# Four interleaved layers on one core: tokens of both parities side by side in a tile, part of the hi/lo split on TensorE, and a schedule written out in tables

## The chip, the cores and the metric

One core of one Trainium2 chip. The metric is device microseconds of one execution; a kernel's time is the median of its runs. The engines are called as in the profile: PE (TensorE matmul), PEld (its weight loads), DVE (VectorE), ACT (ScalarE), POOL (GpSimd) and SP (SyncE, which here only issues DMAs).

## What is computed

S = 2048 tokens of D = 512 features pass through four layers, each with a residual: A, B, A, B, with the same weights for both A and for both B.

```python
def _A_ref(x, wqkv, wo):            # H = 32 heads of 16, W = 8 keys, dilation 2
    q, k, v = split_heads(x @ wqkv)
    idx = pos[:, None] - 2 * arange(8)[None, :]      # keys t, t-2, ..., t-14
    logits = einsum("bhsd,bhswd->bhsw", q, k[idx]) * Dh ** -0.5   # masked where idx < 0
    return einsum("bhsw,bhswd->bhsd", softmax(logits), v[idx]) @ wo
def _B_ref(x, w1, w2, w3, w4):      # F = 1792
    h = gelu(layernorm(x) @ w1)
    g = [h's quarters of features, shifted by +1, -1, +2, -2 tokens]
    x1 = x + concat(g) @ w2
    return x1 + gelu(layernorm(x1) @ w3) @ w4
x = x + _A_ref(layernorm(x)); x = x + _B_ref(layernorm(x))    # twice
```

## The kernel before

**Blocks and tiles.** The tokens are cut into four blocks of 512 (`NB`), each block into four tiles of 128 (`NT`), and there are two layer pairs, so stages run over n = 0 to 7: n = 4*l + b. Tile i of a block holds the tokens 8k + 2i + par (k = 0 to 63, par 0 or 1) of that block. Partition p = 64*par + k: the even ones in the lower half, the odd ones in the upper. A token's eight keys then lie in the same partition or in its neighbours of the same half.

**hi/lo split.** Matmuls run in fp16 with every operand as two halves, an early one (the value rounded to fp16, "hi") and a late one (the rest, "lo"); `HLS` lists the three products hi*hi, hi*lo, lo*hi. So a product with 512 features in takes 12 matmuls of 128x512. Block 0's QKV product and the first MLP (n = 0) are in fp32 instead, because the weights are not split yet.

**Stages.** `p1_stream(n)` normalises a block's tiles, transposes them on PE, splits them and multiplies by the QKV weights; results go through the buffers `ev` (three) to DRAM (`kv_d`, `q_d`). `p2_unit(n, qt)` is the attention of a quarter of the features (8 heads) of a block: it loads q and, for K and for V, 11 slots of 128 features per partition, and works on DVE: a product of 4096 elements per partition, a reduction, the softmax (the exponential on ACT), a second product, three adds. `p3(n)` multiplies by Wo, normalises, transposes and splits, multiplies by W1 and writes the mixer's input `h`, transposed, with short copies on POOL for the shifts across its columns. `p4(n)` multiplies by W2 and normalises, `p5(n)` is the MLP in 14 chunks of 128 of F, with the weights' halves read from DRAM (`w34`), where `big_pair` put them. A tile's transpose and split is `turn_pe` (line 644): four transposes into one PSUM tile, then `split` (line 667): ACT copies the early half out, DVE subtracts it from the PSUM tile and writes the late half.

**Block 0.** Its Q, K and V stay in SBUF: `p1_quarters` writes them there, and `p2_unit` (lines 946 to 966) copies and shifts K and V by SBUF-to-SBUF DMAs, one copy and four shifts for each of K and V and each quarter; the last rows go to `kv_d` for block 1.

**Transfers.** `dma` (line 473) is one DMA from SP; `dma2` (line 477) is two, one for each half of the partitions. Loads of x and of kv and stores of K and V go half by half.

**What sets the order.** Nothing is issued where it is written. Every step is an operation in a graph, `op(key, alts, ...)` (class `Graph`, line 201), with its engine and an assumed duration, or several engines to choose from. `plan` (line 246) runs a small event model: whenever an engine is free, it gives it the ready operation with the lowest key whose buffers are free, and takes the buffers that are free. The keys written in the code are overridden by the table `PLACES` (line 57). An operation that only some engines may do takes the engine that comes free first in that model. The order that results is kept on each engine (`InOrder`, line 348), and each engine runs its queue strictly in order. Since every instruction is issued through `InOrder`, the profile gives them all line 358; the tiles tell them apart.

Some names of tiles in the profile: `xt` the transposed input of QKV, `nT` the transposed input of W1 or W3, `oT` the attention's output transposed, `prod` the attention's products, `L` its logits, `f` normalised tiles, `g` the MLP's middle, `acc` its sums, `mm` the other PSUM tiles (four).

Of the kernel before, what the change touches and what calls it, by code (L numbers as in the profile page):

```python
# [18 lines left out]
P = 128  # L19
# [11 lines left out]
PAD = W - 1  # L31
NSL = NT + W - 1
# [6 lines left out]

# [4 lines left out]


PLACES = [int(k) for k in """
# [127 lines left out]
""".split()]  # L185


class Buf:

# [11 lines left out]
class Graph:  # L201
# [3 lines left out]
    def __call__(self, key, alts, r=(), w=(), after=(), xfer=0.0):  # L205
# [26 lines left out]
        for p in before:  # L232
            p.succ.append(o)
# [1104 lines left out]
```

## Time and profile before

| what | value |
|---|---|
| median of 3 runs | 1242.08 us (1238.16 to 1244.62) |
| span of the profiled execution | 1238.3 us |
| its own time | not given beside the span; the lowest run is 1238.16 us |
| PE / DVE / ACT / POOL busy | 1193.5 / 903.5 / 632.0 / 372.4 us |
| instructions | 15802 |
| moved by DMA | 176.71 MB in 129597 packets |

The span runs from the first to the last instruction. A busy PE may be running at half clock: the column PEclk of a stretch is the mean clock that it was granted, as a share of the full one. In a row of waits stand the total, how often, and the longest. In a row of a timeline stand start, duration, engine, line, operation, tiles, count, and in brackets the idle time before it with what ended it; SPq is a DMA's issue on SP.

### The profile page before, as it was taken

How to read it: one execution, taken by the hardware profiler on the slowest of the kernel's cores; microseconds unless marked ns; L12 is line 12 of the kernel's file. 1: busy time of each engine (PE TensorE's matmuls, PEld its weight loads, DVE VectorE, ACT ScalarE, POOL GpSimd, SP SyncE). 2: the span in 40 equal slices, each digit the busy share in tenths (PEclk: the TensorE clock that was granted, in tenths of full speed). 3: DMA queues.
4: the chain of work that ended last, by engine and by line, in shares of the span. 5: the costliest groups of instructions: out<-in, count | busy, mean ns of one | idle time of the engine just before them, and what ended most of it. 6: DMA issues, size and time to landing. Idle time of an engine off the chain costs nothing.

```text
span 1238.3 us, 15802 instructions
## 1 busy us (share of the span) xinstructions
PE 1193.5 (96%) x5676; PEld 592.2 (48%) x5676; DVE 903.5 (73%) x896; ACT 632.0 (51%) x1108; POOL 372.4 (30%) x516
## 2 busy tenths in 40 slices
PE   9977799899999999999999999989999999999998
PEld 7533344455454445444444545444454444444554
DVE  4776998998999989599954998389855888314212
ACT  4645547533774456556543655365543654444431
POOL 6342123402540264147422252051513432121000
PEclk9988899899999999999999999999999999999999
DMA  6565777586666543653348623764157435211322
GB/s 199 160 163 156 220 219 227 161 227 169 195 178 177 132 136 81 151 154 95 109 147 197 162 75 126 202 153 124 60 153 187 124 93 167 68 60 58 88 85 68
DMA packets 129597, 176.71 MB, mean 143 GB/s; under 512 B 11504, under 2 KB 72912, under 8 KB 129520
## 3 DMA queue, kind: packets, MB, share of 16 engines
q1 hardware_dynamic: 127216, 173.78, 50.2%
q10 hardware_dynamic: 2304, 1.95, 0.6%
q8 instruction: 44, 0.72, 0.3%
q14 instruction: 33, 0.27, 0.1%
HBM read 132.64 MB, written 37.87 MB: 138 GB/s over the span
## 4 chain that ended last, share of the span: by engine, by line
PE 76%; DVE 7%; DMA 7%; ACT 3%; POOL 2%; SPq 2%; issue 2%; ACTq 0%; DVEq 0%; POOLq 0%
PE mm L358 54%; PE acc L358 22%; DVE prod L358 3%; SPq L358 2%; DMA kv<-kv_d 2%; DMA kv<-x 1%; DVE L L358 1%; POOL b L358 1%; DMA w<-in_A_x_dram 1%; POOL a L358 1%; DMA h<-in_B_w_dram 1%; ACT junk L358 1%; DMA q<-q_d 1%; ACT ev L358 1%; DMA kv_d<-ev 1%
## 5 line engine op out<-in xcount | busy, mean ns | idle before, releaser
L358 PE MATMUL acc<-w,g 128*128 128x512 f16 (+1 forms) x1260 | 309.0, 394 | 0.0
L358 PE MATMUL mm<-nT,w 128*128 128x512 f16 (+1 forms) x1288 | 305.5, 390 | 1.5 <-ACT nT L358 0.7
L358 PE MATMUL mm<-wq_hl,xt 128*128 128x512 f16 x1008 | 234.8, 389 | 13.3 <-ACT ev L358 11.4
L358 ACT ACTIVATE mm<-mm,s_w 128x512 f32<-128x512 f32 (+1 forms) x144 | 90.6, 629 | 228.8 <-PE mm L358 228.5
L358 PEld LDWEIGHTS <-w 128*128 128x128 f16 x1344 | 124.9, 98 | 137.3 <-issue 1.3
L358 PEld LDWEIGHTS <-g 128*128 128x128 f16 x1176 | 115.1, 98 | 129.9 <-issue 1.1
L358 PEld LDWEIGHTS <-xt 128*128 128x128 f16 x1008 | 100.3, 100 | 133.8 <-issue 23.2
L358 DVE TENSOR_TENSOR prod<-kv,q 128x4096 f32<-128x4096 f32 x29 | 128.6, 4434 | 20.2 <-DMA kv<-kv_d 12.2
L358 DVE TENSOR_TENSOR prod<-kv,L 128x4096 f32<-128x4096 f32 x32 | 141.4, 4418 | 0.6 <-DMA kv<-kv_d 0.3
L358 DVE TENSOR_REDUCE L<-prod 128x256 f32<-128x4096 f32 x32 | 141.2, 4414 | 0.1
L358 DVE TENSOR_TENSOR prod<-prod 128x2048 f32<-128x2048 f32 x64 | 117.5, 1837 | 1.1
L358 POOL TENSOR_TENSOR g<-f,g 128x512 f16<-128x512 f32 x42 | 61.0, 1453 | 189.7 <-ACT g L358 89.4
L358 DVE SCALAR_TENSOR_TENSOR g<-mm,c_g,g 128x512 f16<-128x512 f32 x56 | 41.8, 747 | 75.8 <-ACT g L358 74.1
L358 PE MATMUL mm<-nT,w_hl 128*128 128x512 f16 x384 | 87.8, 379 | 0.0
L358 PE MATMUL mm<-wo_hl,oT 128*128 128x512 f16 x384 | 86.1, 379 | 0.0
L358 PE MATMUL mm<-w_hl,h 128*128 128x512 f16 x384 | 85.0, 379 | 0.0
L358 POOL COPY h<-h 128x126 f16<-128x126 f16 (+3 forms) x56 | 47.4, 869 | 118.1 <-DVE h L358 116.6
L358 PE MATMUL mm<-ident,f 128*128 128x128 f32 x384 | 59.0, 280 | 21.0 <-ACT f L358 16.0
L358 ACT ACTIVATE g<-mm,c_g 128x512 f16<-128x512 f32 x98 | 66.9, 685 | 2.1
L358 PEld LDWEIGHTS mm<-ident,f 128*128 128x128 f32 x384 | 47.2, 143 | 40.2 <-ACT f L358 19.1
L358 ACT ACT_TABLE_LOAD x48 | 61.6, 1283 | 9.0 <-DVE mx L358 5.2
L358 PEld LDWEIGHTS <-oT 128*128 128x128 f16 x426 | 41.7, 98 | 49.4 <-issue 0.6
(159 smaller groups left out, 1365.0 us busy)
## 6 DMA issues: line engine op xcount, KB each, us to landing
w<-w SPq DMA_DIRECT2D x196, 256.0 KB
kv<-kv_d SPq DMA_DIRECT2D x112, 352.0 KB
w<-in_B_w_dram SPq DMA_DIRECT2D x56, 256.0 KB
kv_d<-ev SPq DMA_DIRECT2D x112, 128.0 KB
x<-x SPq DMA_DIRECT2D x32, 256.0 KB
q_d<-ev SPq DMA_DIRECT2D x28, 256.0 KB
w<-g SPq DMA_DIRECT2D x28, 256.0 KB
q<-q_d SPq DMA_DIRECT2D x28, 256.0 KB
```

Source lines behind the costliest of these rows:

```text
L358: i = f(*a, **k).ins
```

## The change

- **Parities side by side.** Partition p = 2k + par. The rows of a tile of x then are one access pattern, and every transfer that went half by half is one DMA. K, V and Q share one DRAM tensor `kvq_d`, 12 planes (K, V, Q times four quarters), with four rows of zeros ahead of each. A kv load takes 12 slots in three pieces of 512 floats per partition, rows p, p+2 and p+4.
- **Block 0.** Quarters 1 to 3 of its K and V are stored to `kvq_d` and loaded back like those of other blocks; quarter 0 is shifted in SBUF by three DMAs each for K and V.
- **h.** Its columns are permuted so that the shifts are reads of 128 columns next to each other; the writes to the first two quarters become strided by pairs.
- **Split on PE.** `turn_split(minus=True)` multiplies the early half by minus the identity into the PSUM tile with the transposes, and ACT copies the late half out. It is taken for n in `MINUS`: the QKV inputs of n = 1 to 3 and the W1 inputs of n = 0 and 1. Elsewhere the subtraction stays on DVE. A third form by transposing DMA (`turn_dma`) is written but `BY_DMA` is empty.
- **Finer operations, more engines.** The softmax steps and the adds of an attention unit, and the PSUM copies of block 0, are operations of their own; more kinds have two or three engines to choose from.
- **Tables.** `PLACES`, the durations and the event model are gone. `ORDER` lists all 3135 operations (number times 4, plus the engine's place among the alternatives), `SLOTS` gives each buffer its place.
- The statistics of blocks 1 to 3 come ahead of their tiles (`p1_stats`), with one power for four tiles (`powers`). Explicit dependencies, such as Wo after the previous W2, go.

The core of the diff (`...` marks what is left out):

```diff
-PAD = W - 1
-NSL = NT + W - 1
+NSL = NT + W
+BACK = 4
...
+ORDER = [int(k) for k in """
+40 8 12 24 28 1492 32 20 1476 16 56 0 52 4 60 36 64 472 100 48 464 44 468 104 70 80 768 72 776 76 110 84 461 112 488
...
 def plan(ops, slots):
...
+    for b, c in zip(bufs.values(), "".join(SLOTS.split()), strict=True):
+        b.t = slots[b.kind][int(c, 16)]
+    for k in ORDER:
+        o = ops[k // 4]
+        assert o.before | o.order <= done
+        done.add(o)
+        todo.append(o.alts[k % 4][1])
+    assert len(done) == len(ops)
+    return todo
...
-    kv_d = [dram.tile([3, 4, 2, PAD + S // 2, P], F32, name=f"kv_d{l}") for l in range(2)]
-    q_d = [dram.tile([4, NB, P, NT, P], F32, name=f"q_d{l}") for l in range(2)]
+    minus_id = const.tile([P, P], F16, name="minus_id")
+    G.tensor_scalar(minus_id, ident, -1.0, None, ALU.mult)
+    kvq_d = [dram.tile([12, BACK + S // NT, NT * P], F32, name=f"kvq_d{l}") for l in range(2)]
...
+    def turnstile(line, *a):
+        before[line] = [dma(*a, after=before.get(line, ()))]
...
-    def rows(ap, b, i, par):
+    def rows(ap, b, i):
+        v = ap[512 * b + 2 * i:512 * b + 2 * i + 1, 0:D]
+        return at(v, [[8 * D, 64], [D, 2], [1, D]])
...
-        dma2(key, lambda p: par_of(f32v(t.t, D), p), lambda p: rows(x_d, b, i, p), [], [t], 0.8, after)
+        dma(key, lambda: f32v(t.t, D), lambda: rows(x_d, b, i), [], [t], after)
...
+    def turn(key, n, dst, rd):
         ps = Buf("mm")
         def fn():
             for c in range(NC):
                 f = slice(P * c, P * (c + 1))
-                T.transpose(ps.t[:, f], n.t[:, f], ident)
+                T.matmul(ps.t[:, f], n.t[:, f], ident, is_transpose=True, start=(c == 0), stop=(c == NC - 1))
...
+    def turn_split(key, n, dst, cells, hi, lo, rd, scale=None, minus=False):
+        ps, pv = turn(key, n, dst, rd)
+        hc, lc = [(dst, [(c, a) for c in cells]) for a in range(2)]
+        if minus:
+            act(key, lambda: A.activation(hi(), pv(), AF.Copy), [ps], [hc])
+            pe(key, lambda: T.matmul(pv(), minus_id, hi(), start=False, stop=True, skip_group_check=True), [hc], [ps])
+            act(key, lambda: A.activation(lo(), pv(), AF.Copy), [ps], [lc])
+        elif scale is None:
+            act(key, lambda: A.activation(hi(), pv(), AF.Copy), [ps], [hc])
+            dve(key, lambda: V.tensor_sub(lo(), pv(), hi()), [ps, hc], [lc])
...
+    MINUS = (1, 2, 3), (0, 1), ()
+    BY_DMA = (), (), (), ()
...
-                    for par in range(2):
-                        dma(key, lambda i=i, j=j, par=par: at(
-                            kv_d[l][j - 1, 0, par, PAD + 256 * b + i], [[NT * P, 64], [QS, 4], [1, P]]),
...
+                dma(key, lambda i=i, k=k: at(
+                    kvq_d[l][4 * k, BACK + P * b, P * i:P * (i + 1)], [[RS, P], [QS, 4], [1, P]]),
...
+                turnstile("kv", kl + 0.12 * j, lambda j=j: kv[j].t.rearrange("p (s f) -> p s f", s=3),
+                          lambda j=j: at(plane(l, j, qt, P * b), [[RS, P], [2 * RS, 3], [1, RS]]),
+                          [(kvb[l], [(*c, j) for c in cells] + ["pad"])], [kv[j]])
...
+            def to(a, g=g):
+                v = blocks(h.t, HW)[:, a, g]
+                if g < 2:
+                    return at(v[:, 1:], [list(v.ap[0]), [P, NT], [2, 64], [P - 1, 2]])
+                return v[:, P:] if g == 2 else v[:, :D]
...
-                for p in range(2):
-                    dma(base, lambda b=b, i=i, p=p: rows(out_d, b, i, p),
-                        lambda x=x, p=p: par_of(x.t, p), [x], [], 0.4, by_act=n == N - 1 and p == 1)
+                dma(base, lambda b=b, i=i: rows(out_d, b, i), lambda x=x: x.t, [x], [], by_act=n == N - 1 and k % 2)
```

More of the change, by code (lines that the diff above doesn't have):

```diff
@@ L193, in __init__ @@
         self.kind, self.t, self.cells = kind, t, {}
-        self.users, self.left, self.slot = 0, 0, None
 class Op:
-    __slots__ = ("key", "alts", "succ", "n", "est", "touch", "seq", "fn", "end", "xfer", "eng", "lend")
+    __slots__ = ("alts", "before", "order", "touch", "seq")
 class Graph:
@@ L231, in __call__ @@
         before.discard(o)
-        for p in before:
-            p.succ.append(o)
-        o.n = len(before)
+        o.before, o.order = before, set(after)
         o.touch = [b for b in touch.values() if b.kind is not None]
-        for b in o.touch:
-            b.users += 1
-            b.left += 1
         self.ops.append(o)
         return o
-LAT, LAT_PE, LAT_SP, LAT_DMA, TABLE = 0.12, 0.4, 0.3, 2.3, 1.3
 def plan(ops, slots):
-    free = [0.0] * 5
-    pool = {k: [(0.0, j) for j in range(len(v))] for k, v in slots.items()}
+    bufs, done, todo = {}, set(), []
@@ L439, in tile_mixer @@
     V.memset(nhalf, -0.5)
-    maskb = const.tile([P, NT, W], F32, name="maskb")
-    G.memset(maskb, 0.0)
-    for base in (0, 64):
-        for i in range(NT):
-            if i < 3:
-                G.memset(maskb[base:base + 2, i, 0:3 - i], -1e9)
-            G.memset(maskb[base:base + 1, i, 0:7 - i], -1e9)
+    junk = const.tile([P, D], BF16, name="junk")
+    zero = slots["prod"][0][:4 * 8, :D]
+    V.memset(zero, 0.0)
     ident = const.tile([P, P], F32, name="ident")
@@ L468, in tile_mixer @@
+    RS = NT * P
+    QS = (BACK + S // NT) * RS
     kvb = [Buf() for _ in range(2)]
-    qb = [Buf() for _ in range(2)]
     w34 = Buf()
-    def dma(key, out, in_, r, w, xfer, after=(), by_act=False):
-        e, q, d = (ACT, A, 0.6) if by_act else (SP, Y, 0.45)
-        return op(key, [(e, d, lambda: q.dma_start(out(), in_()), None)], r, w, after, xfer)
-    def dma2(key, out, in_, r, w, xfer, after=()):
-        def fn():
-            for par in range(2):
-                Y.dma_start(out(par), in_(par))
-        return op(key, [(SP, 1.15, fn, None)], r, w, after, xfer)
@@ L500, in tile_mixer, with act, dve, gp @@
-    GELU, EXP = "gelu", "exp"
-    xd1 = [dram.tile([P, NT, D], F32, name=f"x1_{b}") for b in range(NB)]
+    def act(key, fn, r, w, cls=None, after=(), also=()):
+        return op(key, [(ACT, fn, cls), *also], r, w, after)
+    def dve(key, fn, r, w, after=(), also=()):
+        return op(key, [(DVE, fn, None), *also], r, w, after)
+    def gp(key, fn, r, w, after=(), also=()):
+        return op(key, [(POOL, fn, None), *also], r, w, after)
+    def pe(key, fn, r, w, after=()):
+        return op(key, [(PE, fn, None)], r, w, after)
@@ new lines, in dma @@
+    def dma(key, out, in_, r, w, after=(), by_act=False):
+        e, q = (ACT, A) if by_act else (SP, Y)
+        return op(key, [(e, lambda: q.dma_start(out(), in_()), None)], r, w, after)
+    before = {}
+    def turnstile(line, *a):
+        before[line] = [dma(*a, after=before.get(line, ()))]
+    GELU, EXP = "gelu", "exp"
+    tiles = list(range(NT))
+    for l in range(2):
+        dma(-8.6, lambda l=l: at(kvq_d[l][0, 0], [[QS, 8], [RS, BACK], [1, RS]]), lambda: zero,
+            [], [(kvb[l], "pad")], by_act=True)
@@ L504, in tile_mixer, with masks @@
+    maskb = keep("maskb", [P, NT, W])
+    def masks():
+        G.memset(maskb.t, 0.0)
+        for i in range(NT):
+            if i < 3:
+                G.memset(maskb.t[0:4, i, 0:3 - i], -1e9)
+            G.memset(maskb.t[0:2, i, 0:7 - i], -1e9)
+    gp(-8.0, masks, [], [maskb])
+    xd1 = [dram.tile([P, NT, D], F32, name=f"res{b}") for b in range(NB)]
     xb = Buf()
@@ L534, in power_of @@
         ps, f2 = Buf("mm"), Buf("mx")
-        pe(key, 0.4, lambda: T.matmul(ps.t[:, :n], ones, ssv, start=True, stop=True), [ss], [ps])
+        pe(key, lambda: T.matmul(ps.t[:, :n], ones, ssv, start=True, stop=True), [ss], [ps])
         def bound():
@@ L542, in bound @@
             V.tensor_scalar(f2.t[:, :m], v, 1e-30, 1e30, ALU.max, ALU.min)
-        dve(key, 0.35, bound, [ps], [f2])
-        p = inv.t[:, :m] if inv.kind is None and not isinstance(inv.t, tuple) else inv.t
-        gp(key, 0.6, lambda: G.tensor_tensor(p, f2.t[:, :m], nhalf[:, :m], ALU.pow), [f2], [inv])
+        dve(key, bound, [ps], [f2])
+        p = inv.t[:, :m]
+        gp(key, lambda: G.tensor_tensor(p, f2.t[:, :m], nhalf[:, :m], ALU.pow), [f2], [inv])
         def cut():
@@ L651, in fn @@
                 f = slice(P * c, P * (c + 1))
-                T.transpose(ps.t[:, f], n.t[:, f], ident)
-        pe(key, 0.44, fn, rd, [ps, (dst, "new"), *new])
-        split(key, ps, dst, cells, hi, lo, scale)
-    def turn_f32(key, n, dst, cell, out):
-        ps = Buf("mm")
-        def fn():
-            for c in range(NC):
-                f = slice(P * c, P * (c + 1))
-                T.transpose(ps.t[:, f], n.t[:, f], ident)
-        pe(key, 0.44, fn, [n], [ps, (dst, "new")])
-        act(key, 0.6, lambda: A.activation(out(), ps.t.rearrange("p (c t) -> p c t", c=NC), AF.Copy), [ps], cell)
@@ new lines, in turn_dma @@
+    def turn_dma(key, n, dst, cells, out, rd, scale=None):
+        hl = Buf("g")
+        hv = lambda a: halves(hl.t)[:, a]
+        sc = 1.0 if scale is None else scale.t
+        k = [] if scale is None else [scale]
+        hc = [(dst, [(c, a) for c in cells]) for a in range(2)]
+        act(key, lambda: A.activation(hv(0), n.t, AF.Copy, scale=sc), rd + k, [(hl, 0), (dst, "new")],
+            also=[(DVE, lambda: V.tensor_scalar(hv(0), n.t, sc, None, ALU.mult), None)])
+        if scale is None:
+            op(key, [(DVE, lambda: V.tensor_sub(hv(1), n.t, hv(0)), None),
+                     (POOL, lambda: G.tensor_sub(hv(1), n.t, hv(0)), None)], [n, (hl, 0)], [(hl, 1)])
+        else:
+            rest(key, lambda: hv(1), lambda: n.t, sc, lambda: hv(0), [n, (hl, 0), scale], [(hl, 1)])
+        op(key, [(SP, lambda: Y.dma_start_transpose(out(), hl.t), None)], [(hl, [0, 1])], hc)
@@ new lines, in p1_stats @@
+    def p1_stats(n, key):
+        l, b = lb[n]
+        tot, ss, ve, r, nb = [s[n % SC] for s in stat["a"]]
+        k = SN ** -2
+        for i in range(NT):
+            x = xs[0, b, i] if l else xin[0, b, i]
+            src = lambda x=x: x.t if l else f32v(x.t, D)
+            if l == 0:
+                act(key, lambda src=src, i=i: A.activation(
+                    junk, src(), AF.Identity, accum_out=tot.t[:, i:i + 1]), [x], [(tot, i)])
+            t = x_sum[b] if l else tot
+            sq_dev(key, src, t, ss, i, [x])
+            if l:
+                power(key, ss, ve, r, i, C1 * k, EPS * k, t, C0, nb)
+        if l == 0:
+            powers(key, ss, ve, r, C1 * k, EPS * k, tot, nb)
@@ L768, in p1_quarters @@
+            for j in range(2):
+                r0 = P - BACK if qt == 0 else 0
+                dma(-4.4 + 0.1 * qt, lambda j=j, qt=qt, r0=r0: at(
+                    plane(0, j, qt, BACK + r0), [[RS, P - r0], [1, RS]]),
+                    lambda kv=kv, j=j, r0=r0, first=first: kv[j].t[r0:P, first:first + RS],
+                    [(kv[j], tiles)], [(kvb[0], [(0, i, qt, j) for i in range(NT)])])
         first_q["done"] = done
@@ L1282, in down @@
                                      start=(c == 0 and j == 0), stop=(c == NF - 1 and j == 2))
-                pe(key, 0.65 * (k1 - k0), down, [w4, (g, [0, 1])], acc[k0:k1])
-        for k, (m, i) in enumerate(tiles):
+                pe(key, down, [w4, (g, [0, 1])], acc[k0:k1])
+        for k, (m, i) in enumerate(grp):
             l, b = lb[m]
@@ L1307, in tile_mixer @@
             p2(n + 3)
[L1308 to L1309 removed]
+    for fn in plan(op.ops, slots):
+        fn()
 _INS = ['A_x', 'A_wqkv', 'A_wo', 'B_w1', 'B_w2', 'B_w3', 'B_w4']
```

656 lines of the change are left out of this document (260 added, 396 removed), and 265 rows, old and new, of tables (ORDER, PLACES).

## The prediction

> **What bounds the kernel now.** I read the page's busy shares first, then the busy time by stretches, then the waits of TensorE (PE), VectorE (DVE) and ScalarE (ACT), then the timelines of the worst stretch.
>
> ```profile
> PE 1193.5 (96%) x5676; PEld 592.2 (48%) x5676; DVE 903.5 (73%) x896; ACT 632.0 (51%) x1108; POOL 372.4 (30%) x516
> ```
>
> ```profile
> core 0: us, PE busy (x) PEld busy (x) DVE busy (x) ACT busy (x) POOL busy (x), PEclk, DMA share, GB/s
> 0.00:40.30 40.30, 37.86 (x193) 28.00 (x194) 18.23 (x36) 21.98 (x57) 19.99 (x52) 1.00 0.66 193
> 40.30:172.90 132.60, 108.80 (x466) 52.43 (x465) 107.80 (x97) 68.64 (x151) 35.53 (x48) 0.92 0.64 174
> 172.90:341.00 168.10, 162.93 (x643) 83.20 (x642) 154.24 (x157) 93.51 (x170) 55.75 (x78) 0.98 0.72 203
> 341.00:1200.00 859.00, 850.15 (x4183) 411.66 (x4181) 615.80 (x596) 440.25 (x715) 261.16 (x339) 1.00 0.46 127
> 1200.00:1238.30 38.30, 33.78 (x201) 16.86 (x198) 7.48 (x13) 7.60 (x16) 0.00 (x0) 0.97 0.23 69
> ```
>
> TensorE is the bound, but not at the start. Of its 44.8 us without work (span less busy), 23.8 lie between 40.3, the first attention product, and 172.9, the first product with Wo; there the granted clock is 0.92, which costs 0.08 x 132.6 = 10.6 us more. From 341 on it is idle for 8.9 us and, at the tail, 4.5. So the start is where time can be won. VectorE rests there too: 132.6 - 107.8 = 24.8 us. What do they wait for?
>
> ```profile
> PE mm L358 <- ACT ev L358: 13.2, 6, 4.2
> ```
>
> ```profile
> ACT ev L358 <- DMA kv_d<-ev: 8.5, 2, 6.0
> ```
>
> ```profile
> 76.09 4.35 SPq L358 DMA_DIRECT2D kv<-x  x5
> ...
> 84.36 4.01 SPq L358 DMA_DIRECT2D x<-in_A_x_dram  x6
> ```
>
> TensorE waits for ScalarE to empty a PSUM tile into `ev` (three buffers), ScalarE waits for the store that empties `ev`, and that store stands in the queue of SyncE (SP), where five shift copies alone take 4.35 us to issue and six loads of x 4.01: 0.67 to 0.87 us each. Issuing is the scarce thing.
>
> ```profile
> kv_d<-ev SPq DMA_DIRECT2D x36, 128.0 KB
> w<-in_A_x_dram SPq DMA_DIRECT2D x32, 128.0 KB
> ...
> kv<-x SPq DMA_DIRECT2D x12, 126.0 KB
> ```
>
> These are the largest counts in 0 to 172.9 us; all SP rows of that view add up to 169.
>
> **Reading the tables.** An entry k of ORDER is operation k//4, in order of creation in the code, taken in its way k%4. Counting the operations through the code names every entry, and rows priced over one engine's entries ahead of a mark say how much that engine must do first. That count is my main tool; it is work, not time, and waits come on top.
>
> **Transfers.** Ahead of the first Wo product SP's entries number 87, against 169: each K or V store is one instead of two (18 fewer), each load of x one instead of two (16 and 5), each kv load one (4), and the first block's 50 shifts, copies and edge stores become 18. At 0.67 to 0.87 us per issue, 82 fewer free 55 to 71 us of SP's queue in a stretch of some 150, so the `ev` stores no longer stand behind it. A kv load grows from 2 x 352 to 768 KB, in pieces of 2 KB. Its nearest price is the slowest load on the chain:
>
> ```profile
> 937.91 8.71 DMA kv<-kv_d
> ```
>
> 9% of that is 0.8 us per load. I take zero: in the table the value load of the third unit of block 0 stands 40 us of VectorE work ahead of its use, and most others 15 us or more. With the cover gone the 62 loads would cost 50 us, most of it after 341, where TensorE has other work queued. The other bound is a gain, the 6.9 us of kv waits shown further down.
>
> **Subtraction on TensorE.** Only 20 of the 128 transposed tiles take it (the QKV inputs of blocks 1 to 3, the mixer inputs of blocks 0 and 1); none goes by transposing DMA, as BY_DMA is empty.
>
> ```profile
> 368.31 2.59 PE acc L358 x12
> ```
>
> ```profile
> 149.40 0.60 PE L358 MATMUL mm<-ident,f 128*128 128x128 f32 x4
> 149.84 0.60 PE L358 MATMUL mm<-ident,o 128*128 128x128 f32 x4
> ```
>
> ```profile
> L358 DVE TENSOR_TENSOR xt<-mm,xt 128x512 f16<-128x512 f32 x29 | 20.0, 689 | 33.4 <-ACT xt L358 33.4
> ...
> L358 ACT ACTIVATE xt<-mm 128x512 f16<-128x512 f32 x29 | 17.2, 594 | 8.3 <-PE mm L358 8.0
> ```
>
> A group of 12 matmuls paces at 2.59 us, so one costs 0.216 and twenty 4.3 us; a tile's four transposes pace at 0.44. VectorE loses 20 x 0.69 = 13.8 us, ScalarE gains 20 x 0.59 = 11.9 (it is half idle). The new wait is on TensorE: the minus matmul waits for ScalarE's early half, and every later matmul stands behind it. For most tiles the table puts a group of 2.59 us between, enough for 0.59. Its price lies between zero and 20 x 4.2 (the longest wait above) = 84 us; nearest is the wait for this same early half now:
>
> ```profile
> PE mm L358 <- ACT xt L358: 1.3, 3, 0.7
> ```
>
> 20 x 0.7 = 14 us. I take zero, since all twenty lie where, as shown next, TensorE has 28 us to spare; without that cover it is 14.
>
> **The sum.** In the new order TensorE cannot pass the third block's first Wo product before VectorE has finished twelve attention units.
>
> ```profile
> 126.88 4.42 DVE L358 TENSOR_TENSOR prod<-kv,x 128x4096 f32<-128x4096 f32 x1
> 131.22 0.75 DVE L358 SCALAR_TENSOR_TENSOR w_hl<-nT,inv_w,w_hl 128x512 f16<-128x512 f32 x1
> ...
> 145.37 3.54 DVE L358 TENSOR_TENSOR prod<-prod 128x2048 f32<-128x2048 f32 x2
> ...
> 149.56 0.42 DVE L358 TENSOR_TENSOR L<-L,maskb 128x256 f32<-128x256 f32 x1
> ```
>
> ```profile
> L358 DVE TENSOR_TENSOR L<-L,mx 128x256 f32<-128x256 f32 x64 | 31.5, 493 | 2.2
> ...
> L358 DVE TENSOR_REDUCE mx<-L 128x32 f32<-128x256 f32 x64 | 26.4, 413 | 2.2 <-ACT L L358 1.9
> ...
> L358 DVE RECIPROCAL mx<-mx 128x32 f32<-128x32 f32 x32 | 11.3, 353 | 1.1
> ```
>
> Start to start a big product costs 4.34 us; two of them and the reduction, as long, make 13.0, the three adds 4.2, the five softmax steps (31.5 + 26.4 + 11.3)/32 = 2.2, the late half 0.7: 20.1 a unit, 241 for twelve.
>
> ```profile
> L358 DVE SCALAR_TENSOR_TENSOR g<-w,inv_p,g 128x512 f16<-128x512 f32 x28 | 20.7, 780 | 0.0
> ...
> L358 DVE SCALAR_TENSOR_TENSOR wq_hl<-h,inv_q,wq_hl 128x1152 f16<-128x1152 f32 x4 | 5.8, 1504 | 0.8 <-ACT wq_hl L358 0.8
> ```
>
> The other 170-odd entries ahead of that mark I estimate from rows like these (wide QKV halves 1.5, weight halves and evacuations 0.7, scalars 0.15): weights 51, evacuations of PSUM moved here 8, normalisations 5, the rest 24, together 88. That is 329 us, of which 27 stand ahead of the first attention product. It comes at 40 as now: TensorE's entries ahead of it are 28.8 us and its first real one starts at 10.9. So VectorE reaches the mark at 40 + 302 = 342 us plus its rests. Between 40.3 and 341 it now rests for 38.7 us (300.7 less 262.0), and the waits split them:
>
> ```profile
> DVE xt L358 <- ACT xt L358: 14.1, 6, 7.3
> DVE mx L358 <- PE mm L358: 5.2, 2, 4.6
> DVE prod L358 <- DMA kv<-kv: 4.5, 1, 4.5
> ...
> DVE inv_w L358 <- POOL inv_w L358: 3.7, 1, 3.7
> ...
> DVE nT L358 <- ACT nT L358: 2.8, 3, 1.5
> DVE prod L358 <- DMA kv<-x: 2.4, 1, 2.4
> ```
>
> The 14.1 and 2.8 belong to subtractions that leave its queue, the 4.5 and 2.4 to shift copies that go. 14.9 remain, of which 8.9 (mx, inv_w) hang on where the weights' scales are placed: between 6 and 15, I take 12. VectorE is at the mark at 354.
>
> ```profile
> 243.92 2.74 PE L358 MATMUL mm<-nT,w 128*128 128x384 f32 x8
> ```
>
> The first MLP's fp32 chunks take about as long as a group (2.74 with the end of the pipeline). TensorE's entries ahead of the mark: 108 groups at 2.59 = 279.7 (28 of them such chunks, 12 fp32 quarters of the first QKV), the first quarter's smaller ones 10.4, 43 transposed tiles 18.9, minus matmuls and sums 5.7: 314.7. From 10.9 on that is 325.6, so it waits 28 us. All its entries make 416 x 2.59 + 56.3 (128 transposed tiles) + 30.1 (small shapes) + 4.3 = 1168, and 853.5 are left after the mark. Behind it I keep the tail of 4.5 us and 6 of the other 8.9, since the table spreads 40-odd evacuations and normalisations to a second engine: 10.5 in all. Sum: 354 + 853.5 + 10.5 = 1218.0, against 1238.3. The same count for the kernel before, 10.9 + 1164 + 43.8 idle + 15 by the clock column, gives 1234, so it closes within 5 us. The profile names no time of its own execution beside its span; the median of the runs, 1242.08, is 3.8 above the span, and I add that: 1221.8, rounded **1222 us**.
>
> **Edits priced at nothing.** The new writes of h (pairs side by side) and the layout of oT move the same elements; if the eight h tiles ahead of the mark doubled a 0.75 us late half, 6 us. Engine choices bring VectorE from 903 to about 950 us in all, still 81% of TensorE. Output as whole tiles leaves the last eviction and its store as they are.
>
> **Rivals.** *VectorE keeps its rests (slower).* The new order ties TensorE to VectorE more tightly: block 2's attention stands ahead of the weights' late halves. If VectorE goes on at its present 262.0 busy of 300.7 us, 302 us take 346.6, the mark comes at 386.6 and the end at 1250.6 + 3.8 = 1254. The point of no gain is 32 us of rest. For it: its longest rest, 7.3, is a head-of-line wait, and a fixed order has those too. Against: the named causes of 24 us are removed. Chance 0.11.
>
> *The start is won and given back.* With 47 us more on VectorE, each of six later blocks could see another wait like TensorE's 4.2 at its worst now, less those I keep: 6 x 2.7 = 16 us, 1238. Chance 0.14.
>
> *GpSimd and VectorE hold each other up.* Both halves are in the trace:
>
> ```profile
> 40.32 4.81 POOL L358 TENSOR_TENSOR a<-a,nhalf 128x1 f32<-128x1 f32 x1
> ```
>
> ```profile
> L358 DVE TENSOR_TENSOR o<-prod x32: 691/692/1679, 73.5 to 1056.0; 128x512 f32<-128x512 f32 x32
> L358 DVE TENSOR_TENSOR prod<-kv,q x29: 4409/4417/4843, 40.3 to 1028.5; 128x4096 f32<-128x4096 f32 x29
> ```
>
> A one-column power took 4.81 us beside a product that began at 40.3, and a 0.69 us add once took 1.68. 76 GpSimd operations stand ahead of the mark, and the attention steps are now cut finer, so GpSimd gets in more often. At 0.99 us a collision, 14 of them bring the gain to the edge of what can be told, 1236, and all 76 give 1297. But the medians lie on the minima, 0.692 and 4.417, so most pass; I put it at 10 to 15 collisions, 1232 to 1237. Chance 0.09. [...]
>
> *More than forecast.* Without rests and with only the tail behind, 342 + 853.5 + 4.5 + 3.8 = 1204. Chance 0.08.
>
> **How the numbers follow.** The forecast has 0.58. Its unknowns: rests 6 to 15 (-6, +3), minus waits (hidden by the 28 spare), strided writes (+6), later loss 4.5 to 13.4 (-6, +3): 1210 to 1234. Leaving out half of the best case and most of the slow one, the range is 1207 to 1243. About 0.5%, 6.2 us, is what a measurement of this kernel can tell, so faster means under 1235.9. Faster: forecast, best case, most of GpSimd's 0.09 and a little of the given back, 0.75; same 0.14; slower 0.11.
>
> **What would show it.** Right: SP issues near 550 in all; in the first 150 us hardly a wait of ScalarE's ev on its store; the first Wo product at 145 to 155 instead of 172.9; VectorE's share from 40 to 341 at 0.95 or more against 0.87; the third block's first Wo product at about 354 with TensorE waiting before it; idle after it at most 13 us. Wrong: VectorE below 0.90 there, waits "PE mm <- ACT xt" of several microseconds at the minus matmuls, kv loads at the head of VectorE's waits, or new idle of TensorE in the last 800 us.

## The result and the profile after

The changed kernel takes 1269.21 us (median of 4 runs, 1268.43 to 1270.26), outside the range that was given. The kernel before takes 1241.67 beside it (4 runs, 1238.16 to 1244.62). The ratio is 1.0229, 95% interval 1.0208 to 1.0250: slower by 2.3%, where 1222 us and faster had been forecast. Its profiled execution has a span of 1267.5 us.

First the page's busy shares and the busy time by stretches of the changed kernel, over the stretches shown of the kernel before (all instructions of the new file have line 281):

```profile
PE 1202.0 (95%) x5696; PEld 594.1 (47%) x5696; DVE 955.1 (75%) x1008; ACT 585.6 (46%) x986; POOL 382.9 (30%) x480
```

```profile
0.00:40.30 40.30, 37.57 (x195) 27.64 (x196) 28.64 (x62) 17.20 (x46) 12.35 (x36) 1.00 0.66 210
40.30:172.90 132.60, 119.50 (x547) 60.74 (x546) 123.03 (x128) 73.28 (x149) 39.86 (x45) 0.95 0.71 224
172.90:341.00 168.10, 156.13 (x590) 78.29 (x589) 157.79 (x142) 80.07 (x125) 48.59 (x55) 0.96 0.49 157
341.00:1200.00 859.00, 826.36 (x4010) 396.42 (x4009) 633.72 (x659) 399.20 (x634) 282.09 (x345) 0.99 0.41 132
1200.00:1267.50 67.50, 62.47 (x361) 31.04 (x359) 11.88 (x21) 15.89 (x32) 0.00 (x0) 1.00 0.22 71
```

The start is won: between 40.3 and 172.9 TensorE (PE) is idle for 13.1 us instead of 23.8, at a clock of 0.95 instead of 0.92. Behind it the gain is lost: idle is 12.0 us instead of 5.2 in the next stretch, and 32.6 instead of 8.9 from 341 to 1200. A new wait does it, the first of TensorE's waits:

```profile
PE mm L281 <- DVE h L281: 25.3, 10, 4.5
```

TensorE waits for VectorE (DVE) to write h, the mixer's input. That wait was not there before. The rows of tile h (min/median/max ns, first and last start, forms) show why; first the kernel before, then after:

```profile
L358 ACT ACTIVATE h<-mm,c_h x32: 667/687/700, 201.8 to 1112.9; 128x512 f16<-128x512 f32 x32
L358 DVE SCALAR_TENSOR_TENSOR h<-mm,c_h,h x32: 734/744/751, 207.9 to 1113.6; 128x512 f16<-128x512 f32 x32
```

```profile
L281 ACT ACTIVATE h<-mm,c_h x32: 668/1601/2567, 180.4 to 1100.1; 128x512 f16<-128x512 f32 x32
L281 DVE SCALAR_TENSOR_TENSOR h<-mm,c_h,h x32: 737/1611/2647, 183.0 to 1100.8; 128x512 f16<-128x512 f32 x32
```

The shapes are the same, the count is the same, and half of the writes, 16 of 32 on each engine, take 2.5 us instead of 0.7: a median that lies midway between minimum and maximum says that there are two kinds. The slow ones are those of the first two quarters, which now go to h pair by pair. The timeline of the first block shows what one of them holds up:

```profile
179.38 0.66 ACT L281 ACTIVATE mm<-mm,s_w 128x512 f32<-128x512 f32 x1
...
180.44 2.54 ACT L281 ACTIVATE h<-mm,c_h 128x512 f16<-128x512 f32 x1
...
183.01 2.48 DVE L281 SCALAR_TENSOR_TENSOR h<-mm,c_h,h 128x512 f16<-128x512 f32 x1 [1.65 <-ACT h L281]
...
185.55 2.75 PE L281 MATMUL mm<-nT,w_hl 128*128 128x512 f16 x12 [2.16 <-DVE h L281]
```

Gelu, early half on ScalarE (ACT) and late half on VectorE stand one behind the other, and the PSUM tile stays taken through all three: from the gelu to the end of the late half 6.1 us, where 0.66 + 0.69 + 0.74 = 2.1 us of work was there before. There are four such tiles. When they are taken, TensorE stands still, here for the 2.16 us of the last row. The longer queue of VectorE seems to count as well: TensorE's waits for two other tiles that VectorE writes, mx (5.3 us) and o (3.1), shrink to 0.6 and to none in the run split below.

After the three longest of the ten stops (4.54, 3.80 and 3.31 us) TensorE also ran on at a lower clock: a group of twelve matmuls that takes 2.75 us took 4.64, 4.44 and 4.44. The clock granted in the first of them, from 762 to 765, was 0.50, and that in the second 0.62 (the third number from the end of the second row below). After one of 3.25 us it did not, and in the run early_split (below) a stop of 2.38 us was followed by a group of 4.21, so the length of the stop alone does not decide it.

```profile
901.94 4.44 PE L281 MATMUL mm<-nT,w_hl 128*128 128x512 f16 x12 [3.80 <-DVE h L281]
```

```profile
901.94:906.38 4.44, 4.44 (x13) 1.66 (x13) 4.41 (x3) 0.00 (x0) 2.35 (x3) 0.62 0.00 0
```

### The profile page after: what moved, and what is told of

Read it like the earlier page. It is cut to its first block, busy times and chain, and to the rows that moved or that the text cites. A ratio compares the mean times of both kernels' runs of the same rounds, so it can differ in the third digit from the quotient of the medians.

```text
span 1267.5 us, 15539 instructions
## 1 busy us (share of the span) xinstructions
PE 1202.0 (95%) x5696; PEld 594.1 (47%) x5696; DVE 955.1 (75%) x1008; ACT 585.6 (46%) x986; POOL 382.9 (30%) x480
## 3 DMA queue, kind: packets, MB, share of 16 engines
q1 hardware_dynamic: 139880, 179.65, 44.4%
## 4 chain that ended last, share of the span: by engine, by line
PE 70%; DVE 15%; DMA 6%; ACT 5%; issue 2%; POOL 1%; SPq 0%; DVEq 0%; ACTq 0%; POOLq 0%
PE mm L281 52%; PE acc L281 18%; DVE prod L281 6%; DVE h L281 3%; ACT h L281 2%; DVE L L281 2%; DMA w<-in_B_w_dram 1%; DMA kv<-kvq_d 1%; DMA kvq_d<-ev 1%; DMA kv<-kv 1%; DVE x L281 1%; DMA q<-kvq_d 1%; DVE g L281 1%; ACT junk L281 1%; ACT mm L281 1%
## 5 line engine op out<-in xcount | busy, mean ns | idle before, releaser
L281 PE MATMUL mm<-wq_hl,xt 128*128 128x512 f16 x1008 | 226.4, 380 | 3.6 <-DVE ev L281 1.8
L281 POOL TENSOR_TENSOR g<-f,g 128x512 f16<-128x512 f32 x42 | 80.9, 1927 | 203.1 <-ACT g L281 120.2
L281 PE MATMUL mm<-nT,w_hl 128*128 128x512 f16 x384 | 95.2, 403 | 20.6 <-DVE h L281 15.7
L281 POOL TENSOR_SCALAR b<-b 128x1 f32<-128x1 f32 (+1 forms) x48 | 37.6, 784 | 170.4 <-ACT junk L281 168.2
L281 DVE SCALAR_TENSOR_TENSOR h<-mm,c_h,h 128x512 f16<-128x512 f32 x32 | 51.4, 1619 | 32.2 <-ACT h L281 31.9
L281 PEld LDWEIGHTS <-w_hl 128*128 128x128 f16 x384 | 39.5, 103 | 71.9 <-issue 33.2
L281 POOL COPY h<-h 128x252 f16<-128x252 f16 (+3 forms) x38 | 29.5, 790 | 139.2 <-DVE h L281 119.1
L281 ACT ACTIVATE nT<-mm 128x512 f16<-128x512 f32 (+1 forms) x71 | 41.6, 592 | 59.9 <-PE mm L281 59.9
```

The lines of the kernel that those rows point to most:

```text
L281: i = f(*a, **k).ins
```

## Experiments

**Theory A**: the pair-wise writes of h are long and hold TensorE up. **Rival B**: the order written out in the tables ties TensorE to VectorE, whatever h costs. **Rival C**: GpSimd (POOL) and VectorE hold each other up, and that makes the writes long.

### Straight writes (contig)

```diff
-                if g < 2:
-                    return at(v[:, 1:], [list(v.ap[0]), [P, NT], [2, 64], [P - 1, 2]])
-                return v[:, P:] if g == 2 else v[:, :D]
+                return v[:, P:] if g % 2 == 0 else v[:, :D]
...
-        k = 2 if g < 2 else 1
+        k = 1
```

> The first two quarters of h are written straight, and shifted by two tokens like the last two, so this is not the reference's mixer; all operations, engines and the order are those of the changed kernel. Theory A (the pair-scattered writes of h hold the PSUM tiles of the W1 product, and TensorE waits for them): the late half on VectorE falls from a mean of 1.62 to 0.75 us, TensorE's waits on h from 25.3 to under 5 us, the third block's first Wo product comes at 353 to 358 instead of 366.1, and the time is 1228 to 1240. Rival B (the written-out order ties TensorE to VectorE, whatever h costs): the waits move to other tiles, 1255 to 1268. Rival C (GpSimd and VectorE hold each other up, which makes these writes long): the late half stays well above 0.75 us, 1260 or more.

Measured: 1223.69 us, ratio to the kernel before 0.9849 (0.9822 to 0.9876), below even the 1228 to 1240 that theory A gave. The late half is at 0.744, TensorE's waits on h are 2.5 us, and the third block's first Wo product moves from 366.1 to 353.3.

```profile
L281 DVE SCALAR_TENSOR_TENSOR h<-mm,c_h,h x32: 731/744/751, 180.1 to 1053.6; 128x512 f16<-128x512 f32 x32
```

```profile
PE mm L281 <- DVE h L281: 2.5, 2, 2.2
```

Around that product, first the changed kernel, then this one:

```profile
40.30:366.12 325.82, 299.84 (x1255) 150.99 (x1254) 302.37 (x301) 166.77 (x301) 104.81 (x113) 0.96 0.59 187
366.12:1267.50 901.38, 864.62 (x4249) 415.50 (x4247) 624.06 (x646) 401.67 (x639) 265.73 (x331) 0.99 0.39 125
```

```profile
40.30:353.27 312.97, 297.05 (x1254) 150.87 (x1253) 295.20 (x301) 159.52 (x301) 111.88 (x113) 0.97 0.61 194
353.27:1220.20 866.93, 855.56 (x4249) 414.05 (x4247) 604.54 (x646) 379.95 (x639) 266.08 (x331) 1.00 0.40 130
```

Of the 47.3 us between the two spans, 12.9 lie ahead of the product (VectorE busy 7.2 longer, which is four long late halves, and resting 5.7 longer) and 34.5 behind it (TensorE idle for 36.8 instead of 11.4, and 9.1 us more busy time for the same 4249 matmuls, at a clock of 0.99 instead of 1.00). Theory A holds; B and C had it at 1255 or more.

### The same columns, parity by parity (split)

```diff
-                    return at(v[:, 1:], [list(v.ap[0]), [P, NT], [2, 64], [P - 1, 2]])
+                    return [at(v[:, 1 + (P - 1) * r:], [list(v.ap[0]), [2, D // 2]]) for r in range(2)]
...
-                return ps.t.rearrange("p (i k r) -> p i k r", i=NT, r=2) if g < 2 else ps.t
+                return [at(ps.t[:, r:], [list(ps.t.ap[0]), [2, D // 2]]) for r in range(2)] if g < 2 else [ps.t]
```

> The same columns are written as in the changed kernel, in two instructions, one for each parity: 256 elements each, every second column, no jump from one element to the next. If the jump of 254 bytes between neighbouring elements is what costs (A1), each takes about 0.45 us, 0.9 for a tile instead of 2.5, and the time is 1232 to 1246. If writing every second column costs as much (A2), each takes 1.2 to 1.3 us, and the time stays at 1265 to 1272. Rival B: 1255 to 1268 with short writes.

Measured: 1226.43 us, ratio 0.9868 (0.9843 to 0.9894), 3.5% below the changed kernel's ratio with every value in the same place, and below the 1232 to 1246 that was expected for A1. Its rows of h:

```profile
L281 ACT ACTIVATE h<-mm,c_h x48: 522/550/690, 180.2 to 1057.2; 128x256 f16<-128x256 f32 x32, 128x512 f16<-128x512 f32 x16
L281 DVE SCALAR_TENSOR_TENSOR h<-mm,c_h,h x48: 487/504/751, 181.2 to 1057.9; 128x256 f16<-128x256 f32 x32, 128x512 f16<-128x512 f32 x16
```

Two instructions of 0.50 us write what one of 2.5 us wrote. So it is A1: not every second column is dear, but the jump from each element to the next (254 bytes forward, then 250 back). This version beats both kernels.

### The writes by themselves (micro)

Every form four times, from PSUM, on ScalarE and VectorE in turn; the tile's name tells the form (a_ ScalarE, v_ VectorE, g_ GpSimd from SBUF).

> Only the disputed writes, each four times and by themselves, GpSimd almost idle; no mixer and no output but zeros. Theory A: the scattered write of 512 fp16 elements takes 2.4 to 2.6 us on ScalarE and on VectorE, against 0.7 straight, with nothing beside it. Rival C: by itself it takes at most 0.9 us. The forms with only the output, only the second input or only the PSUM source out of line tell which operand it is; I expect the output.

The groups of this kernel by form, the costliest first (count, busy us, mean ns, idle before); wronly jumps only in the output, rdonly only in the second input, readps only in PSUM, and stride writes every second element:

```profile
L95 POOL CAST g_scatter<-src 128x512 f16<-128x512 f32 x4 | 10.3, 2570 | 0.0
...
L87 ACT ACTIVATE a_scatter<-ps,scal 128x512 f16<-128x512 f32 x4 | 10.1, 2528 | 8.6 <-DVE v_scatter L88 7.7 <-DVE v_plain L88 0.9
...
L88 DVE SCALAR_TENSOR_TENSOR v_scatter<-ps,scal,early 128x512 f16<-128x512 f32 x4 | 10.0, 2493 | 10.1 <-ACT a_scatter L87 10.1
L88 DVE SCALAR_TENSOR_TENSOR v_wronly<-ps,scal,early 128x512 f16<-128x512 f32 x4 | 9.9, 2484 | 10.4 <-ACT a_wronly L87 10.4
...
L95 POOL CAST g_plain<-src 128x512 f16<-128x512 f32 x4 | 3.5, 878 | 0.0
...
L88 DVE SCALAR_TENSOR_TENSOR v_stride<-ps,scal,early 128x512 f16<-128x512 f32 x4 | 3.2, 788 | 2.3 <-ACT a_stride L87 2.3
L88 DVE SCALAR_TENSOR_TENSOR v_rdonly<-ps,scal,early 128x512 f16<-128x512 f32 x4 | 3.1, 787 | 0.1
L88 DVE SCALAR_TENSOR_TENSOR v_readps<-ps,scal,early 128x512 f16<-128x512 f32 x4 | 3.0, 751 | 3.0 <-ACT a_readps L87 3.0
L88 DVE SCALAR_TENSOR_TENSOR v_plain<-ps,scal,early 128x512 f16<-128x512 f32 x4 | 3.0, 750 | 2.4 <-ACT a_plain L87 2.3
L87 ACT ACTIVATE a_plain<-ps,scal 128x512 f16<-128x512 f32 x4 | 2.7, 687 | 2.6 <-DVE v_plain L88 2.6
```

It is the output alone: jumping in the output costs 2.48 us, jumping in the second input 0.79, PSUM read parity by parity 0.75, every second column without a jump 0.79. All three engines come to the same 2.5 to 2.6 us. VectorE's late ones ran when GpSimd had long ended, as two timeline rows show, and took as long: rival C is out as the cause of the long writes. The price belongs to fp16 outputs here: in the same kernel VectorE copies with an fp32 output jumped as many elements in 0.62 to 0.63 us in their two shortest rows, where the shortest straight one took 0.67.

```profile
47.07 1.54 POOL L95 CAST g_stride<-src 128x512 f16<-128x512 f32 x1
```

```profile
92.35 2.48 DVE L88 SCALAR_TENSOR_TENSOR v_wronly<-ps,scal,early 128x512 f16<-128x512 f32 x1 [2.60 <-ACT a_wronly L87]
```

So the distance between neighbours counts for the fp16 writes (254 bytes apart 2.49 us, 4 bytes apart 0.79) and not for the reads of the second input (254 bytes apart 0.79 us). The reason for it no run shows.

### The jump in the kernel before (before_jump)

```diff
+                if g < 2:
+                    return at(v[:, OWN[g]:], [list(v.ap[0]), [1, D // 2], [D // 2, 2]])
```

> The kernel before, with only the writes of the first two quarters of h made to jump (512 bytes between neighbouring elements, the columns in another order, so the mixer's shifts are not the reference's). Theory A: both halves rise to about 2.5 us a tile and the time from 1242 to between 1255 and 1275. Rival B (it takes the new order to be hurt by it): the writes are as long, but the time is 1242 to 1248.

Measured: 1260.72 us, ratio 1.0140 (1.0104 to 1.0176), 17 us more than the kernel before. Its late halves of h have a median of 1.61 us as in the changed kernel, but TensorE hardly waits for h:

```profile
PE mm L358 <- ACT f L358: 23.6, 12, 5.9
...
PE mm L358 <- DVE h L358: 3.9, 4, 1.6
```

It waits for normalised tiles f that ScalarE makes; that wait was 16.0 us before. Of the 7.6 us more, 1.6 lie ahead of the first write of h. The largest piece is one wait of 5.32 us that was 1.80 before, and ScalarE's long early halves are not what it runs back to: the tile f waits for a power on GpSimd, the power for statistics of the residual x, and x stands in VectorE's queue behind two long late halves, the second of them shown:

```profile
464.62 2.47 DVE L358 SCALAR_TENSOR_TENSOR h<-mm,c_h,h 128x512 f16<-128x512 f32 x1
...
466.70 0.91 DVE L358 SCALAR_TENSOR_TENSOR x<-acc,s_w,x 128x512 f32<-128x512 f32 x1
...
474.65 0.81 ACT L358 ACTIVATE f<-x,a,a 128x512 f32<-128x512 f32 x1 [3.20 <-POOL a L358]
...
475.51 1.11 PE L358 MATMUL mm<-ident,f 128*128 128x128 f32 x4 [5.32 <-ACT f L358]
```

So the writes cost in either order, and the new one pays some 45 us (2.3% + 1.3%) where the old one pays 17, with jumps of 512 bytes that take as long (2.48 to 2.56 us in micro). That much of B is true: the new order has less slack behind these tiles.

### One engine at a time (early_split, late_split)

In split, ScalarE's early halves or VectorE's late halves alone.

> The changed kernel, with only the early halves (ScalarE) of the first two quarters of h written parity by parity; the late halves on VectorE still jump (2.5 us). Both together took 43 us off. Theory L (what counts is how long a PSUM tile is held by gelu, early half and late half one after the other): each alone shortens that by about 1.45 us of 7, and brings about half, 1240 to 1255. Theory V (what counts is VectorE's own load, 16 x 1.5 = 24 us more): this one brings little, 1256 to 1267.

> The other one: only the late halves on VectorE are written parity by parity, the early halves on ScalarE still jump. Theory L: about half, 1240 to 1255. Theory V: most of it, 1227 to 1239.

Measured: early halves mended 1253.68 us, ratio 1.0091 (1.0067 to 1.0114), 17 us off the changed kernel; late halves mended 1245.15, ratio 1.0019 (0.9999 to 1.0039), 26 us off; by the ratios both together 45. TensorE's waits on h, in this order:

```profile
PE mm L281 <- DVE h L281: 17.7, 11, 2.8
```

```profile
PE mm L281 <- DVE h L281: 10.6, 7, 2.3
```

Both times lie in the ranges of theory L and outside those of theory V, so VectorE's load alone is not the cause. That the holding of the PSUM tile is the whole cause is not shown either: 17 and 26 add up to nearly the 45 of both, as links of one chain would, but so would the added load of two engines. The late half counts more than L's two equal links had it, which fits the waits on mx and o above.

### Two DMAs for one (two_dmas, two_x_stores, two_kv)

```diff
+    def dma2(key, out, in_, r, w, after=()):
+        return op(key, [(SP, lambda: [Y.dma_start(part_of(out(), m), part_of(in_(), m)) for m in range(2)], None)],
+                  r, w, after)
```

> Undoes one part on top of the version with both halves split (1226): each load of x from the input, each kv load and each store of K and V is issued as two DMAs, one for each half of the partitions, as in the kernel before; 43 more issues ahead of the first Wo product. Theory of the prediction (issuing on SP is what is scarce at the start): the first Wo product moves from 143.3 to 149 or later, ScalarE's ev waits for its stores again by 5 us or more, and the time is 1231 to 1241. Rival (the shift copies of the first block and the place of the loads in the queue were the cause, not the number of issues): 1224 to 1229, first Wo product within 3 us.

Measured: 1264.28 us, ratio 1.0176 (1.0157 to 1.0194), 38 us more than split, dearer than the 1231 to 1241 expected; the first Wo product moved to 161.2, and ScalarE's ev waits for its stores again, 4.7 us in the first 150 us. The other two runs take it apart.

> Splits the 38 us that the halved transfers cost (1264 against 1226): here only the loads of x from the input and the stores of K and V go as two DMAs, 39 of the 43 additional issues ahead of the first Wo product; kv loads are whole. Theory (issues on SP are what costs): most of the 38 us, 1250 to 1264, first Wo product at 155 to 161. Rival (transfers of 64 partitions land later, above all the big kv loads): 1228 to 1240.

> The other part: only the kv loads go as two DMAs, four more issues ahead of the first Wo product and 62 in all. Theory (issues on SP): 1226 to 1234, first Wo product within 4 us of 143.3. Rival (halved loads land later and their products wait): 1240 to 1258.

Measured: x loads and stores halved 1243.26, ratio 1.0013 (0.9992 to 1.0034), first Wo product at 155.6; kv loads halved 1248.64, ratio 1.0054 (1.0034 to 1.0073), first Wo product at 148.1. So 18 us come from halving the small transfers, whose 39 issues ahead of that product the prediction had counted, and 23 from halving the kv loads, where it had put a whole load at nothing. For the latter there are only four more issues ahead of that product. Halving also costs time on the 16 DMA engines. Queue 1 of the DMA section, split and then two_kv:

```profile
q1 hardware_dynamic: 139880, 179.65, 45.4%
```

```profile
q1 hardware_dynamic: 140872, 179.65, 52.3%
```

The same 179.65 MB take 0.454 x 1224.5 = 556 us of each of the 16 DMA engines, and 0.523 x 1246.8 = 652 when the 62 kv loads go by halves of the partitions, 96 us more (0.470 x 1242.0 = 584 with x loads and stores halved). SP, too, is slower to issue two halves than one whole; in the first 60 us a whole load takes it 0.37 us, both times, and a pair of halves 1.33 and 1.25:

```profile
33.98 0.37 SPq L281 DMA_DIRECT2D kv<-kvq_d  x1
```

```profile
33.92 1.33 SPq L281 DMA_DIRECT2D kv<-kvq_d  x2
```

Both expectations were half right: two_x_stores fell between its two ranges, and two_kv came at the time of the rival but not by its way. VectorE's waits for kv loads are 11.8 us in two_kv and 11.9 in split; TensorE's waits for w_hl (11.7 instead of 7.8) and for ScalarE's writes of nT (6.1 instead of 1.5) grew in their place, and 17.8 of the 22.3 us of span lie ahead of the third block's first Wo product. By which path the halved loads cost these stays open. So does what an order made for halves would lose: the tables were made for whole transfers.

### Subtraction back on VectorE (dve_sub)

```diff
-            pe(key, lambda: T.matmul(pv(), minus_id, hi(), start=False, stop=True, skip_group_check=True), [hc], [ps])
-            act(key, lambda: A.activation(lo(), pv(), AF.Copy), [ps], [lc])
+            pe(key, lambda: None, [hc], [ps])
+            dve(key, lambda: V.tensor_sub(lo(), pv(), hi()), [ps, hc], [lc])
```

> Undoes another part on top of the version with both halves split (1226): the twenty late halves that the minus matmul prepares are subtracted on VectorE again, at the place in the order where ScalarE copied them. VectorE gets 20 x 0.69 = 13.8 us more ahead of the third block's first Wo product, TensorE loses 4.3. If TensorE waits for VectorE there, as the prediction has it, that product comes at 362 to 368 instead of 352.2, and the time is 1233 to 1242. If the minus matmul only moved work that was hidden anyway, the time is 1221 to 1229.

Measured: 1246.46 us, ratio 1.0029 (1.0015 to 1.0043): 20 us more than split, above the expected 1233 to 1242. The third block's first Wo product came at 368.8, 16.6 later for 13.8 us of work, and TensorE waited for the subtractions:

```profile
PE mm L281 <- DVE xt L281: 10.9, 7, 4.5
...
PE mm L281 <- DVE nT L281: 6.3, 3, 2.8
```

Part of this may be that the subtraction stands where the order had put ScalarE's copy, behind VectorE's long products; an order made for it was not run.

### Less work on VectorE (fewer_dve), one wait less on TensorE (pow_later)

```diff
+ON_ACT = (172, 465, 152, 479, 180, 756, 781, 265, 269, 271, 1277, 1263, 252, 313, 289, 309)
+ORDER = [k // 4 * 4 if k // 4 in ON_ACT else k for k in ORDER]
```

> On the version with both halves of h split (1226), sixteen operations ahead of the third block's first Wo product go from VectorE to ScalarE at the same places of the order: six evacuations of K, V and Q, five early halves of weights, five sums of squares, about 0.7 us each, 11 to 12 us of VectorE. If VectorE's work sets when TensorE passes that product, as the sum of the prediction has it, the product comes 6 to 11 us before 352.2 and the time is 1215 to 1221. If ScalarE, in order, takes these late and holds up what stands behind them, the product gains less than 3 us and the time is 1224 to 1235.

Measured: 1227.97 us, ratio 0.9886 (0.9870 to 0.9903), no gain over split. The stretch up to the third block's first Wo product, split and then this one:

```profile
40.30:352.19 311.89, 294.20 (x1256) 148.98 (x1255) 296.18 (x305) 160.77 (x305) 110.78 (x113) 0.98 0.62 195
```

```profile
40.30:355.70 315.40, 296.08 (x1256) 150.11 (x1255) 286.74 (x284) 170.52 (x326) 104.36 (x113) 0.97 0.61 193
```

VectorE has 9.4 us less to do and rests 13.0 us longer, mostly on ScalarE, which now comes later in its own queue:

```profile
DVE oT L283 <- ACT oT L283: 5.2, 3, 2.2
DVE h L283 <- ACT h L283: 4.0, 3, 3.0
DVE xt L283 <- ACT xt L283: 3.0, 1, 3.0
```

Adding work to VectorE moves the product out (dve_sub, and the long writes themselves); taking work from it and giving it to ScalarE did not bring it in, as the second of the two expectations had it.

> On the same version (1226), the sum of squares of W1 on ScalarE and the small matmul and the power behind it are moved a few entries back, so that TensorE does not stand for 6.2 us at 61.5 to 67.6 waiting for a weight that is still loading. If idle time of TensorE ahead of the third block's Wo product is covered by VectorE, as the prediction has it, 4 to 6 us of idle go and the time stays at 1223 to 1229. If TensorE's own idle there reaches the end, 1219 to 1222.

Measured: 1226.19 us, ratio 0.9871 (0.9850 to 0.9893), and the product at 352.05 instead of 352.19. The time stayed, as expected, but not for the reason given: the wait for w_hl fell from 7.8 to 1.2 us, and that for the normalised tile behind it rose from 2.7 to 8.6. One wait took the other's place, and TensorE was idle for 18.6 us ahead of that product instead of 17.7, so this does not show whether its idle time there is covered.

```profile
PE mm L291 <- POOL f L291: 8.6, 3, 5.9
```

## Why the prediction was wrong, point by point

**The step that failed** is "Edits priced at nothing": "The new writes of h (pairs side by side) and the layout of oT move the same elements; if the eight h tiles ahead of the mark doubled a 0.75 us late half, 6 us." The same elements moved, but the time of an fp16 write went by where each element lands (in micro 0.75 us straight, 2.48 jumping). The factor was 3.3 (3.7 on ScalarE) instead of at most 2; it fell on ScalarE's early half as well as VectorE's late half; it fell on all 16 tiles of these two quarters, not only on those ahead of the mark; and it was priced as VectorE's load ahead of the mark, not as time for which a PSUM tile is held and TensorE waits, before the mark and after it. As that load alone the bound came out nearly right, and by luck: only four of the eight tiles grew, but each by more than twice as much, 7.2 us against 6. Counted fully, 16 x (1.75 + 1.84) = 57 us of work on two engines, it became 25 us of waits of TensorE on h, its slower clock after some of them and a later mark: 47 us of span, 34.5 of them behind the mark, where the prediction had put nothing for it. The row for a jump was not in the trace of before, where all writes of h are straight; the bound from above had to be wider for it.

**The sum itself** held. With straight writes the time is 1223.7, with the reference's columns 1226.4, against 1222:

| term | forecast | changed kernel | straight writes | split |
|---|---|---|---|---|
| first Wo product | 145 to 155 | 143.1 | 142.4 | 143.3 |
| VectorE busy, 40.3 to the mark | 302 | 302.4 | 295.2 | 296.2 |
| its rests there | 12 | 23.4 | 17.8 | 15.7 |
| mark (third block's first Wo product) | 354 | 366.1 | 353.3 | 352.2 |
| from the mark to the end | 864 | 901.4 | 866.9 | 872.3 |
| of it TensorE idle | 10.5 | 36.8 | 11.4 | 13.0 |

VectorE's work was put 6 to 7 us too high without the long writes and its rests 4 to 6 too low; the two cancel, which is luck. In the changed kernel the 302 is met by accident, with 7 us of long writes in it. Behind the mark split takes 8 us more than forecast: TensorE is busy for 859.4 us instead of 853.5 and idle 2.5 longer. The 3.8 us beside the span were 1.7 in the changed kernel (1269.21 less 1267.5) and 1.9 in split. So split meets the total partly because these misses have opposite signs.

**The start** went as forecast: ScalarE's ev has no wait on its store in the first 150 us, SP issues 551 transfers by the DMA section of the profile instead of 740, and the first Wo product comes 30 us earlier. The 169 and 87 issues ahead of it are in the two traces, though the savings that the prediction lists add up to 75 and not 82. The cause was named only in part: small transfers issued once instead of twice are worth 18 us, whole kv loads, which the text held at zero with only their added bytes in view, 23 (both in an order made for whole ones). The sum did not miss it because it counted work up to a mark and did not add up differences.

**The minus matmul** was priced rightly: TensorE waited 1.9 us in all for ScalarE's halves of xt and 0.9 for those of nT. Taking it back costs 20 us, more than the 13.8 of VectorE's work, with the reservation made above.

**TensorE's spare 28 us** ahead of the mark are there in split (17.7 idle, and 0.02 x 311.9 = 6.2 by the clock), but that VectorE's amount of work alone sets the mark fell with fewer_dve. What would bring the mark in further stays open.

**Rivals.** "The start is won and given back" had the right course and the wrong mechanism and size: its six waits of 2.7 us were to come from VectorE's load over the later blocks, 16 us in all, and h alone made ten waits and 25.3 us. "VectorE keeps its rests" did not happen as such: its share between 40.3 and 341 was 0.934, below the 0.95 named and above 0.90. GpSimd against VectorE: the first product's group has a mean of 4.50 us over a median of 4.42 in the changed kernel, 2.3 us over 29, so most still pass. The sign named as wrong, "new idle of TensorE in the last 800 us", is the one that showed.

## What to carry to other kernels

Price a changed access pattern like a changed instruction: count, shape and type can all stay, and the order of an fp16 output alone more than trebled the time here (0.75 to 2.48 us on VectorE in micro). When a layout is chosen so that reads become straight, look at what its writes do between one element and the next, walk them so that neighbours stay near each other, even in two instructions (here two of 0.50 us for one of 2.5), and price a longer PSUM eviction by how long the tile is held along its whole chain and by what stands behind it in its engine's queue. And use a whole transfer over all partitions where two halves were: here halved kv loads cost both issue time (1.33 and 1.25 us against 0.37) and a sixth more DMA engine time (652 us against 556).

## What the runs showed of the hardware that was not expected

In micro, writing 512 fp16 elements per partition took 0.69 to 0.88 us in a straight line and 2.5 to 2.6 us when each landed 250 or 254 bytes from the last, on ScalarE and VectorE from PSUM and on GpSimd from SBUF (there with copies of the other two beside it) alike; reading such a pattern as the second input cost 0.04 us, and reading PSUM parity by parity nothing (0.751 against 0.750). With an fp32 output VectorE showed no such price (0.62 against 0.67 in the shortest rows). A kv load of 768 KB was issued in 0.37 us, its two halves together in 1.25 to 1.33 (two rows of each).
